# Moving GpSimd's first queue drain from ahead of the fourth slot's gathers to behind them

## The chip, the core and the metric

The kernel runs on one core of one Trainium2 chip. The metric is the device time of one launch in microseconds (us), as the median of several runs; the profile comes from one further execution. Six engines matter here: TensorE (PE, with its weight loads PEld), VectorE (DVE), ScalarE (ACT), GpSimd (POOL), SyncE (SP) for the plain DMA transfers, and the 16 DMA engines. GpSimd issues the indirect transfers (gathers and scatters) itself.

## What is computed

Attention with a sigmoid in place of the softmax, and then a mixture of eight experts that sends each token to one expert:

```python
scores = scale * q @ k.T - log(S);  attn = 1 / (1 + exp(-scores))
x = (attn @ v)                         # 8 x 448 tokens = 3584 rows of 768
e_idx = argmax(x @ w_gate)             # one expert of 8 for each token
h  = maximum(x[mask] @ w1[e], 0)       # 768 -> 1024
out[mask] = gate_w * sigmoid(x @ w_output_gate)[e] * (h @ w2[e])   # 1024 -> 768
```

All values are float32 at the interface.

## The kernel before

Attention and routing come first (about 300 us). For every token the routing writes a row of six words into a list in DRAM, sorted by expert; each expert's list is cut into tiles of 256 tokens. The second part works through these tiles, one *slot* for each: `slot(m)`, m from 0. The first `EARLY` = 3 slots take tokens whose attention ends early; the slot with m = 3, the fourth, is the last that always runs. The slots after it (same function, m > 3), the three wide slots and the two half slots of this run stand under branches.

A slot holds two layers. In layer 1 PE multiplies the 256 tokens by the expert's w1 in eight column blocks f; numbers are split into a high and a low part, so that block f takes twelve matmuls, L576 with the high and L577 with the low weights in turn, over six row pieces d = 0 to 5. In layer 2 (L601 to L603) it multiplies by w2, in four parts (t, n): two token halves t, two column halves n. From m = 3 on the last part is finished in the next slot (`finish`, at f = 6 there).

Three things are prepared while PE works, and they set the order on the other engines:

- **Tokens.** `gather` (L496 on, the DMA at L501) issues eight indirect DMAs on GpSimd, each of which fetches 128 quarter rows into `xg`, a single buffer of the pool `plain`. In slot m the gathers are for slot m + 2. `turn_x` (L558) lets DVE transpose `xg` into `xT`; it waits for all eight gathers, and the next slot's gathers wait for it. `split_x` then makes high parts on ACT and low parts on DVE (L532 and L533, from 128x512 tiles).
- **Weights.** `high_w1(k)` (ACT, L536) and `low_w1(k)` (DVE, L539), k = 0 to 2, split w1 for the next slot; piece k serves d = 2k and 2k + 1. On ACT the order at a slot's end is: high_w1(0), split_x, output (0,0), high_w1(1), output (0,1), high_w1(2), output (1,0).
- **Results.** `layer2_out` (L621) scales a part on ACT into `ys[0]` or `ys[1]` (half t), and after the second part GpSimd scatters the buffer to `out` by indirect DMA (L623). ACT's next write to the same buffer waits for that scatter to land.

Everything is in an order written by hand, engine by engine: each engine runs its own list from the top and waits only on semaphores. GpSimd's sequencer runs ahead of the GpSimd cores; a drain stops it there until the DMAs issued before have retired. `nc.gpsimd.drain()` stands in each slot after the fourth at its start (L631), in the wide slots (L685) and the half slots (L717); the first of all is in slot m = 3 (L645). Ahead of this first one GpSimd has issued 87 DMAs: two at the start, 32 that write lists, 40 gathers, seven that read lists, six scatters. In the fourth slot GpSimd also unpacks the lists of the late slots (`spread_lists`, `spread_rest`, L461 to L487), which ends just ahead of that drain.

Of the kernel before, what the change touches and what calls it, by code (L numbers as in the profile page):

```python
# [35 lines left out]
EARLY = -(-(ROWS_E - E * (TS - 1)) // TS)  # L36
# [22 lines left out]
class Kernel:  # L59
# [567 lines left out]
    def slot(self, m, side=None):  # L627
        tab, k = (self.tab_e, m + 1) if m + 1 < EARLY else (self.tab_l, m + 1 - EARLY)
        nx = self.load_slot(tab, k, self.lists(m + 1))
        if m > EARLY:  # L630
            self.nc.gpsimd.drain()  # L631
        self.split_w2(0)
        for f in range(8):
            if m > EARLY and f == 6:
                self.finish()
            self.layer1(f, m == 0 and f == 0)
            if f:
                self.high_low(f - 1)
            if f in (1, 3, 5):
                self.split_w2(f // 2 + 1)  # L640
            if side is not None and f < 7:
                next(side, None)
        self.high_low(7)
        if m == EARLY:
            self.nc.gpsimd.drain()  # L645
        self.load_w2(nx)
        self.high_w1(0)
        self.turn_x(nx)
        if m == 0:
            next(side, None)  # L650
        if m == 1:
            next(side, None)
        self.gather(self.lists(m + 2), ROWS_E if m + 2 < EARLY else NT)
        for k in range(3):
            self.split_x(nx, k)
        self.low_w1(0)
        for i, (t, n) in enumerate(((0, 0), (0, 1), (1, 0), (1, 1))):
            if i == 3 and m >= EARLY:
                self.layer2_due(self.lists(m), 1)
            else:  # L660
                ps = self.psy[(0, 1, 3)[i] if m >= EARLY else (4 * m + i) % 3]
                self.layer2(self.lists(m), t, n, self.ys[t], ps)
            if i < 2:
                self.split_w1(i + 1)
            if side is not None and i > 0:
                for _ in range(3 if m == 0 and i == 1 else 1):
                    next(side, None)
# [380 lines left out]
```

## Time and profile before

| What | us |
|---|---|
| median of three runs | 783.53 (783.46 to 785.43) |
| profiled execution | 785.01 |
| its span, first to last instruction | 783.3 |
| time around the span | 1.7 |
| PE busy | 767.6 (98%) |
| DVE / ACT / GpSimd busy | 497.8 / 488.1 / 353.9 |
| slot m = 3 (PE, layer 1 to layer 2) | about 383 to 416 |
| slot m = 4 | about 416 to 449 |

The granted clock of TensorE is 1.00 in all 20 us stretches from 300 to 740. To read the views: a timeline row has the start in us from the start of the span, the duration in us, the engine, the source line, the operation, output and input tiles, and in brackets how long the engine stood idle before and what ended it. An idle time "<-issue" is one in which the profile saw nothing to wait for. POOLq is GpSimd's sequencer, where drains are recorded.

### The profile page before, as it was taken

What the parts mean: (1) busy time and instruction counts of PE and PEld (TensorE: products, weight loads), DVE (VectorE), ACT (ScalarE), POOL (GpSimd) and SP (SyncE); (2) the same over time, 40 slices, a digit from 0 to 9 for tenths busy, and PEclk for the clock granted to TensorE, in tenths of its full rate; (3) what the DMA queues carried; (4) which work ended last, traced back from release to release, by engine and by line L of the source; (5) the groups of instructions that cost most, each with busy time, mean ns of one, the idle gap of its engine ahead of it and who ended that gap; (6) DMA issues with size and microseconds to landing.
All of it is one profiled execution on the core that took longest, in us unless ns stands there. A gap on an engine that the chain in (4) does not pass through costs nothing. (4 is left out here: it accounts for less than half of the span.)

```text
span 783.3 us, 15087 instructions
## 1 busy us (share of the span) xinstructions
PE 767.6 (98%) x5724; PEld 561.6 (72%) x5724; DVE 497.8 (64%) x800; ACT 488.1 (62%) x662; POOL 353.9 (45%) x464
## 2 busy tenths in 40 slices
PE   9999999999999999999999999999999999999896
PEld 4333433333443369899999989999899999889685
DVE  2334444443456768876786576858577685787677
ACT  5666666666668757565675565746556474675585
POOL 4003301230331676778895667255372643633522
PEclk9999999999999999999999999999999999999999
DMA  6352544445258550147666497511156655856771
GB/s 252 142 212 91 195 165 173 159 143 213 81 204 303 191 184 12 53 176 238 232 201 249 160 343 280 182 51 42 40 223 204 259 158 210 315 212 237 278 307 46
DMA packets 37616, 145.23 MB, mean 185 GB/s; under 512 B 5639, under 2 KB 7791, under 8 KB 33552
## 3 DMA queue, kind: packets, MB, share of 16 engines
q1 hardware_dynamic: 27696, 119.56, 42.6%
q0 software_dynamic: 9824, 24.46, 9.3%
q8 instruction: 51, 0.84, 0.4%
q14 instruction: 45, 0.37, 0.2%
HBM read 152.61 MB, written 23.05 MB: 224 GB/s over the span
## 5 line engine op out<-in xcount | busy, mean ns | idle before, releaser
L800 ACT ACTIVATE a<-ps,bias_s 128x896 f32<-128x896 f32 x168 | 169.1, 1008 | 96.6 <-PE ps L798 96.6
L576 PE MATMUL ps<-rounded 128*128 128x512 f32 (+1 forms) x672 | 225.9, 386 | 1.7 <-PEq L990 1.2
L501 POOL DMA_INDIRECT plain<-x_dram,lxs x122 | 181.9, 1491 | 65.2 <-issue 40.5
L577 PE MATMUL ps<-rounded 128*128 128x256 f32 (+1 forms) x672 | 184.1, 274 | 1.4 <-DVE rounded L539 1.2
L798 PE MATMUL ps<-kqv 64*64 64x448 f32 x1344 | 157.9, 541 | 0.4 <-ACT a L800 0.4
L807 PE MATMUL ps<-a,kqv 64*64 64x448 f32 x1344 | 156.8, 536 | 0.0
L601 PE MATMUL ps<-w2h,h 128*128 128x384 f32 x432 | 144.9, 335 | 0.0
L533 DVE TENSOR_TENSOR w2l<-plain,w2h 128x1536 fp32r<-128x1536 f32 x60 | 105.2, 1757 | 62.0 <-ACT w2h L532 61.4
L602 PE MATMUL ps<-w2l,h 128*128 128x384 f32 x432 | 144.4, 334 | 0.0
L603 PE MATMUL ps<-w2h,h 128*128 128x384 f32 x432 | 144.4, 334 | 0.0
L576 PEld LDWEIGHTS ps<-rounded 128*128 128x128 f32 x672 | 125.8, 187 | 25.0 <-issue 3.0
L577 PEld LDWEIGHTS ps<-rounded 128*128 128x128 f32 x672 | 127.2, 189 | 2.3 <-DVE rounded L539 2.0
L807 PEld LDWEIGHTS ps<-a,kqv 64*64 64x64 f32 x1344 | 51.6, 133 | 75.3 <-issue 74.2
L539 DVE TENSOR_TENSOR rounded<-plain,rounded 128x2048 fp32r<-128x2048 f32 x46 | 103.3, 2284 | 1.8 <-ACT rounded L536 1.8
L798 PEld LDWEIGHTS ps<-kqv 64*64 64x64 f32 x1344 | 48.7, 133 | 74.0 <-issue 60.7
L532 ACT CAST w2h<-plain 128x1536 fp32r<-128x1536 f32 x60 | 88.1, 1472 | 19.3 <-PEq L995 6.3
L584 ACT COPY gl<-ps 128x256 f32<-128x256 f32 (+1 forms) x112 | 40.3, 360 | 93.9 <-PE ps L577 87.0
L536 ACT CAST rounded<-plain 128x2048 fp32r<-128x2048 f32 x46 | 87.3, 1903 | 0.0
L601 PEld LDWEIGHTS ps<-w2h,h 128*128 128x128 f32 x432 | 81.1, 188 | 2.3 <-issue 1.8
L602 PEld LDWEIGHTS ps<-w2l,h 128*128 128x128 f32 x432 | 81.1, 188 | 0.1
L603 PEld LDWEIGHTS ps<-w2h,h 128*128 128x128 f32 x432 | 81.1, 188 | 0.0
L623 POOL DMA_INDIRECT out<-y,due x11 | 18.3, 1666 | 117.6 <-ACT gl L584 92.4
(209 smaller groups left out, 716.5 us busy)
## 6 DMA issues: line engine op xcount, KB each, us to landing
plain<-w SPq DMA_DIRECT2D x68, 768.0 KB
plain<-w SPq DMA_DIRECT2D x48, 1024.0 KB
kqv<-kqv SPq DMA_DIRECT2D x23, 1344.0 KB
x_dram<-xt SPq DMA_DIRECT2D x8, 1344.0 KB
plain<-w SPq DMA_DIRECT2D x6, 512.0 KB
plain<-x_dram,lxs POOLq DMA_INDIRECT x122, 5.0
kqv<-kqv SPq DMA_DIRECT2D x1, 896.0 KB
lst<-plain POOLq DMA_DIRECT2D x1, 726.0 KB, 7.2
```

The lines of the kernel that those rows point to most:

```text
L501: self.nc.gpsimd.indirect_dma_start(out=s["xg"][:, g], out_offset=None, in_=x4, in_offset=bass.IndirectOffsetOnAxis(ap=s["lx"][:, g:g + 1] ...
L532: self.nc.scalar.copy(hi, raw)
L533: self.nc.vector.tensor_tensor(lo, raw, r32(hi), ALU.subtract)
L539: self.nc.vector.tensor_tensor(self.w1p[1][k], self.w1r[:, 2 * k:2 * k + 2], r32(self.w1p[0][k]), ALU.subtract)
L576: nc.tensor.matmul(out, wh[d][:, c], both, start=(d == 0), stop=False)
L577: nc.tensor.matmul(ps[:, 0:n], wl[d][:, c], self.xc[:, d, 0, 0:n], start=False, stop=(d == 5))
L601: nc.tensor.matmul(ps, hh[:, f, tk], wh, start=(f == 0), stop=False)
L602: nc.tensor.matmul(ps, hh[:, f, tk], wl, start=False, stop=False)
L603: nc.tensor.matmul(ps, hl[:, f, tk], wh, start=False, stop=(f == 7))
L798: nc.tensor.matmul(ps[half[h], j, 0:S], kg[half[j], e, 0, o:o + 64], kg[half[j], e, 1], start=True, stop=True)
L800: nc.scalar.activation(at[u % 4], ps[:, :, 0:S], AF.Sigmoid, bias=self.bias_s, scale=1.0 / math.sqrt(D))
L807: nc.tensor.matmul(self.ps_o[e][h][half[j], 0:S], v[half[h], 6 if i == 3 else 3 * e + c, j], a[half[h], j], start=(i in ((0, 3 if h else 4 ...
```

## The change

Within `slot`, for m == 3 alone, the drain moves down past `load_w2`, `high_w1(0)`, `turn_x` and `gather`. Of these only `gather` issues on GpSimd, so on that engine the drain changes place with eight indirect DMAs; every other engine's list stays as it was.

```diff
         self.high_low(7)
-        if m == EARLY:
-            self.nc.gpsimd.drain()
         self.load_w2(nx)
         self.high_w1(0)
         self.turn_x(nx)
...
         self.gather(self.lists(m + 2), ROWS_E if m + 2 < EARLY else NT)
+        if m == EARLY:
+            self.nc.gpsimd.drain()
         for k in range(3):
             self.split_x(nx, k)
```

On GpSimd this is the order from the end of the list unpacking (`gl1`, `lts`) through the fourth slot's eight gathers (into `plain`, from `x_dram`) and its scatter (`out` from `y0`) to the fifth slot's first instructions. A drain is not listed, so the rows read the same in both kernels.

```order
L486 TENSOR_SCALAR gl1_105<-lts_100 32x10
L487 COPY gl1_105<-lts_100 32x10
L501 DMA plain_130<-x_dram_62,lxs_101 128x192 [waits DVE_49,Pool_49]
L501 DMA plain_130<-x_dram_62,lxs_101 128x192 x7
L623 DMA out<-y0_2465,lts_100 3584x768 [waits DMASW7_49,Activation_49]
L990 COMPARE_AND_BRANCH
L623 DMA out<-y1_2466,due_99 3584x768 [waits DMASW0_49,DMASW7_49,DVE_49,Activation_49]
```

Before, the first drain stands between L487 and the first L501; now it stands between the last L501 and the first L623. The drain of the fifth slot stands behind L990 in both.

On ACT this is the end of the fifth slot (m = 4), the same in both kernels: its high parts of w1 (L536) and x (L532 from 128x2x256), and the outputs of its layer 2 (L621).

```order
L536 CAST rounded_126<-plain_130 128x2048 [waits DMAHW2_49]
L532 CAST rounded_126<-plain_130 128x2x256 [waits DVE_49]
L532 CAST rounded_126<-plain_130 128x2x256 x2
L621 ACTIVATE y0_2465<-ps_134,lts_100 128x384 [waits DMASW7_49,PE_49]
L536 CAST rounded_126<-plain_130 128x2048 [waits DMAHW3_49]
L621 ACTIVATE y0_2465<-ps_134,lts_100 128x384 [waits PE_49]
L536 CAST rounded_126<-plain_130 128x2048 [waits DMAHW4_49]
L621 ACTIVATE y1_2466<-ps_134,lts_100 128x384 [waits DMASW0_49,PE_49]
```

Nothing moved here. DMASW7, for which the first L621 waits, is the semaphore of the fourth slot's scatter, the L623 from `y0` in the rows above.

## Rows read from the trace of the kernel before

**Rows 1.** The page's first line.
```profile
span 783.3 us, 15087 instructions
```
**Rows 2.** Timeline of PE, first block of slot m = 5.
```profile
450.18 0.39 PE L576 MATMUL ps<-rounded 128*128 128x512 f32 x1
450.72 0.39 PE L577 MATMUL ps<-rounded 128*128 128x256 f32 x1
...
451.29 0.40 PE L576 MATMUL ps<-rounded 128*128 128x512 f32 x1
452.92 0.39 PE L577 MATMUL ps<-rounded 128*128 128x256 f32 x1 [1.23 <-DVE rounded L539]
```
**Rows 3.** Timeline of DVE, ends of slots m = 3 and m = 4.
```profile
402.75 1.78 DVE L558 STREAM_TRANSPOSE plain<-plain 128x1536 f32<-128x1536 f32 x1
...
441.90 1.78 DVE L558 STREAM_TRANSPOSE plain<-plain 128x1536 f32<-128x1536 f32 x1 [7.11 <-DMA plain<-x_dram,lxs]
444.37 1.89 DVE L533 TENSOR_TENSOR rounded<-plain,rounded 128x512 fp32r<-128x512 f32 x3 [0.69 <-ACT rounded L532]
446.18 6.69 DVE L539 TENSOR_TENSOR rounded<-plain,rounded 128x2048 fp32r<-128x2048 f32 x3
```
**Rows 4.** Timeline of GpSimd, slots m = 3 and m = 4.
```profile
403.04 1.02 POOL L623 DMA_INDIRECT out<-y,lts  x1 [0.16 <-DVE h L590]
...
418.92 0.19 POOL L487 COPY gl<-lts 32x10 f32<-32x10 f32 x1
427.14 2.37 POOL L501 DMA_INDIRECT plain<-x_dram,lxs  x1 [8.03 <-issue]
...
439.10 0.94 POOL L501 DMA_INDIRECT plain<-x_dram,lxs  x1 [0.30 <-issue]
440.35 1.01 POOL L623 DMA_INDIRECT out<-y,lts  x1 [0.30 <-issue]
444.81 1.12 POOL L623 DMA_INDIRECT out<-y,due  x1 [3.46 <-ACT rounded L532]
446.24 3.08 POOL L501 DMA_INDIRECT plain<-x_dram,lxs  x1 [0.31 <-issue]
```
**Rows 5.** The drains at L645, L631 (fifth slot's), L685 (first): ns min/median/max, starts.
```profile
L645 POOLq DRAIN  x1: 8314/8314/8314, 418.0 to 418.0; - x1
...
L631 POOLq DRAIN  x1: 9682/9682/9682, 434.1 to 434.1; - x1
...
L685 POOLq DRAIN  x1: 1015/1015/1015, 661.6 to 661.6; - x1
```
**Rows 6.** Issue to landing: the fourth slot's scatter, the fifth slot's, the fourth's gathers.
```profile
DMA to landing us min/median/max: 3.1/3.1/3.1
...
DMA to landing us min/median/max: 8.0/8.0/8.0
...
DMA to landing us min/median/max: 2.6/5.3/6.3
```
**Rows 7.** Timeline of GpSimd, slot m = 1, first and last of eight gathers.
```profile
354.80 1.11 POOL L501 DMA_INDIRECT plain<-x_dram,lxs  x1
...
368.59 0.95 POOL L501 DMA_INDIRECT plain<-x_dram,lxs  x1 [0.30 <-issue]
```
**Rows 8.** Timeline of ACT, end of slot m = 4.
```profile
445.28 0.58 ACT L621 ACTIVATE y<-ps,lts 128x384 f32<-128x384 f32 x1
...
448.03 1.90 ACT L536 CAST rounded<-plain 128x2048 fp32r<-128x2048 f32 x1
```
**Rows 9.** Timeline of DVE: two low parts of w2 (L533).
```profile
422.72 1.76 DVE L533 TENSOR_TENSOR w2l<-plain,w2h 128x1536 fp32r<-128x1536 f32 x1 [0.93 <-ACT w2h L532]
...
661.93 1.76 DVE L533 TENSOR_TENSOR w2l<-plain,w2h 128x1536 fp32r<-128x1536 f32 x1 [0.89 <-ACT w2h L532]
```
**Rows 10.** Timelines of DVE and PE: slot m = 5's last low part, slot m = 6's layer 1.
```profile
479.00 2.29 DVE L539 TENSOR_TENSOR rounded<-plain,rounded 128x2048 fp32r<-128x2048 f32 x1 [0.29 <-ACT rounded L536]
...
484.70 0.39 PE L576 MATMUL ps<-rounded 128*128 128x512 f32 x1
```

## The prediction

> **What bounds the kernel now.** I began with the page: the span is 783.3 us [rows 1], and PE is busy for 98% of it, so only a place where PE stands still can be worth time. The view of waits gives PE just one wait of over 0.3 us on another engine's result from 300 us on: on DVE's low part of w1, in the first block of slot m = 5. PE's timeline shows what it costs. Undisturbed, an L577 follows its L576 after 0.23 us. Here the one at 450.72 comes 0.54 after its L576, and the next but one, at 452.92, comes 1.63 after [rows 2]: 0.31 + 1.40 = 1.7 us lost. That is the most that this stall can give back.
>
> Backwards from there. The L577 at 452.92 needs the third low_w1, the last of three L539 that run back to back from 446.18 to 452.87 [rows 3]. These stand behind split_x, and this behind turn_x, which DVE starts at 441.90 after 7.11 us of idle time, waiting for the gathers [rows 3]. The gathers are issued from 427.14 to 440.04, behind 8.03 us of idle time that the profile puts down to nothing [rows 4]. The record of GpSimd's sequencer fills that gap: the drain L645 starts at 418.0 and lasts 8.314 us, to 426.31 [rows 5]. The transpose that the gathers also wait for (turn_x of the slot before) had ended at 404.53 [rows 3]. So the drain delays the gathers, and by this chain PE loses 1.7 us.
>
> **What the drain itself costs.** GpSimd was busy until 419.11 (418.92 + 0.19) [rows 4], so the drain held it for 7.2 us, although every earlier DMA had landed: the last scatter was issued at 403.04 [rows 4]. In the first wide slot a drain, also with nothing in flight, takes 1.015 us [rows 5]; ten DMAs had been issued since the drain before it (eight gathers, two scatters). 87 DMAs and 7.2 us, ten and 1.0: both fit some 83 ns for each DMA to be retired and about 0.2 us besides. I take the drain for a walk over all DMAs since the last one. The fifth slot's drain shows that the walk need not start after the last landing: it ends at 434.1 + 9.68 = 443.78 [rows 5], 0.3 us after the scatter of 440.35 landed (+ 3.1) [rows 4, 6], although it had nine DMAs to retire.
>
> **The change part by part.** One drain changes place with eight gathers; the other lists stay.
>
> Removed: 7.85 us ahead of the gathers. They may start at some 419.3, which is 419.11 and the 0.2 us that a gather needs behind GpSimd's own copies. Issuing eight took 12.9 us here (427.14 to 440.04 [rows 4]), and 14.7 in slot m = 1 (354.80 to 369.54 [rows 7]), where each gather that met DVE's L533 took about 2.4 us. From 419 to 433 such L533 run as in that slot (the first at 422.72 [rows 9]), so I take 14.7: issued by 434.0, 6 us earlier than now. Their landing, 2.6 to 6.3 us after issue [rows 6], is then at about 436 to 439, and turn_x, split_x and the first low_w1 all run some 4 us earlier than now.
>
> Added: the same drain behind the gathers, now with 95 DMAs to retire: 7.2 x 95/87 = 7.9 us, from 434.0 to 441.9. The gathers land meanwhile, so no wait for them is left over. A gather came 0.83 us after L645's end, the fifth slot's first scatter 1.03 after L631's; with 0.8 the fourth slot's scatter L623 is issued at 442.7, where it is at 440.35 now [rows 4]. What is queued behind the drain on GpSimd is just this scatter, the fifth slot's drain, the scatter from `due` and the fifth slot's gathers; all come some 2.4 us later.
>
> Who waits for them: ACT's output (0,0) of slot m = 4 writes the buffer that this scatter reads. It runs at 445.28 now [rows 8], in its turn behind split_x, and the scatter has landed by 443.45 [rows 4, 6], so that today this wait costs nothing. With the change it lands at 442.7 + 3.1 = 445.8. ACT, ready some 4 us earlier, then stands at this output until 445.8, and high_w1(1) and high_w1(2) stand behind it. From there the chain is: 4.65 us from the output's start to the end of the second high_w1 (445.28 to 449.93 [rows 8]), 2.25 for the third low_w1 (a third of 6.69 [rows 3]), and 0.1 for two hand-overs. That is 445.85 + 7.0 = 452.85 for the L577 that runs at 452.92 now: 0.1 us gained. The end of PE's stall would be set by the scatter in place of the gathers, at nearly the same time.
>
> Behind that, the fifth slot's gathers start at 448.6 in place of 446.24 and are all issued by about 464. The last low part that depends on them ends at 481.29, and PE needs layer 1 of slot m = 6 only from 484.70 on [rows 10], so 2.4 us are covered there; without that cover they would be lost whole. From slot m = 6 on GpSimd waits for ACT, and the delay is gone. The w1 transfer that follows the first low_w1 starts earlier too, on SP's queue, and may crowd the scatter a little: I add 0.2 us for this, an estimate from landings of 3.1 and 8.0 [rows 6], at the near end, since the transfer starts about when the scatter does.
>
> Sum: -0.1 + 0.2 = +0.1 us on the profiled execution's 785.01 (783.3 of span and 1.7 around it). That execution was 1.5 us over the median of the runs, 783.53; put on the median, the forecast is 783.6 us.
>
> Bounds. Eight gathers: 12.9 to 15.7 us (446.24 on, the fifth slot's), -1.8 to +1.0. Drain: if those 7.2 us were no walk and a drain here costs 1.0, the stall ends before it begins, -1.7 in all; the other end is the second rival. Landing: 3.1 to 8.0, up to +4.9. For each I take the value nearest by place: the slot with the same DVE work, the same drain, the scatter itself.
>
> **The rivals.**
> *The drain is cheap there.* If the 7.2 us are something that stands at that point once (code that is fetched, say) and doesn't move with the drain, or if the walk gets through the old DMAs while the gathers are issued, the scatter goes out in time and the stall goes altogether: 783.53 - 1.7 = 781.8. For it: there is only one long drain to look at. Against it: the 1.0 us for ten DMAs scales to it well.
>
> *Slower: DVE shuts the drain out.* GpSimd's gathers double in time beside an L533, which reads two operands. If the walk suffers the same, it loses the 4.2 us of two-operand work that DVE has between 434 and 442 (three L533, 1.89, and one L539, 2.2 [rows 3]). The 7.2 us then hold 1.8 of such shut-out (the L533 at 422.72 [rows 9]), so the walk alone is 5.4 x 95/87 = 5.9, and with 4.2 it is 10.1: 2.2 us more than I took, 783.6 + 2.2 = 785.8. It decides if the drain takes more than about 9 us behind its last gather. Against it: the drain of 1.015 us at 661.6 [rows 5] ended at 662.6, in the middle of an L533 that began at 661.93 [rows 9]. The Trainium skill, SBUF — State Buffer, "Who interferes with whom", says that a DVE instruction with two SBUF inputs blocks a GpSimd instruction that reads SBUF, and not one that only writes. By that rule the time would be 785.8 if the walk reads SBUF, and 783.6 if it doesn't; the row at 661.6 speaks for the latter.
>
> *The scatter lands late.* With w1's transfers in the queues the next slot's scatter took 8.0 us to land [rows 6]. The same here is +4.9, 788.4. Against it: the transfer can start only after the first low_w1, at about 443, when the scatter is out.
>
> **How the numbers follow.** An exchange of one wait for another, at -1 to +1.5 us: 0.60. The stall goes (-1.7): 0.17. DVE shuts the drain out (+2.2): 0.12. The scatter lands late (up to +4.9): 0.06. Something I don't see: 0.05. 0.3%, what a measurement of this kernel can tell from no change, is 2.35 us: the band is 781.2 to 785.9. The first two cases lie inside it, so faster gets 0.04; half of the third and all of the fourth pass it, slower gets 0.13; same 0.83. The range takes in the stall's going and the shut-out drain with a little more for slow gathers: 781.8 to 786.4. The likeliest case's own range is 782.5 to 785.0.
>
> **What would show it.** Right: L645's successor, now L653, lasts about 8 us past its last gather, gathers run from 419 to 434, turn_x no longer waits 7.1 us, ACT's output (0,0) near 445 waits for DMA or for GpSimd where it now follows split_x, and PE still stands 1 to 3 us in that block. Wrong: PE without a stall there (cheap drain), a drain much over 8 us behind the last gather (shut out), or a new stall of PE in slots m = 5 or 6, which would mean that the cover there was too thin.

## The result, and the profile after

The changed kernel takes 791.9 us (median of six runs, 790.06 to 794.24) where the kernel before took 783.94 beside it: the ratio is 1.0095, with an interval of 1.0075 to 1.0115. It is slower by some 8 us, where 783.6 was forecast. The profiled execution took 794.24 us.

The page's first line of the changed kernel, the counterpart of [rows 1]:

```profile
span 792.5 us, 15087 instructions
```

**Where the time went.** I took the first L576 of each slot from PE's timeline in both traces. Up to slot m = 5 they differ by 0.4 us at most. Slot m = 5 takes 43.1 us in place of 35.2, and the slots m = 6 to 9 take 33.3 in both. So 7.9 us are lost in slot m = 5. The two spans differ by 9.2; most of the rest lies behind slot m = 9, in a part whose length varies from kernel to kernel (see a2). A slot without a stall takes 33.28 us: before, slot m = 5 lost 1.9 us, now it loses 9.8.

**GpSimd did what was forecast.** Its timeline, the counterpart of [rows 4], with the last copy, the last gather and the fourth slot's scatter, and the records of the drains L653 and L631 (ns, start), the counterpart of [rows 5]:

```profile
419.27 0.19 POOL L487 COPY gl<-lts 32x10 f32<-32x10 f32 x1
...
431.38 2.39 POOL L501 DMA_INDIRECT plain<-x_dram,lxs  x1 [0.30 <-issue]
442.67 2.81 POOL L623 DMA_INDIRECT out<-y,lts  x1 [8.90 <-issue]
```
```profile
L653 POOLq DRAIN  x1: 19635/19635/19635, 422.1 to 422.1; - x1
...
L631 POOLq DRAIN  x1: 8790/8790/8790, 442.5 to 442.5; - x1
```

The gathers end at 431.38 + 2.39 = 433.8 (forecast 434.0), the drain ends at 422.1 + 19.6 = 441.7 (441.9), the scatter is issued at 442.67 (442.7). But the issue takes 2.81 us, where it took 1.01 before [rows 4], and what follows is new: its landing, the counterpart of [rows 6], is 8.6 us in place of 3.1.

```profile
DMA to landing us min/median/max: 8.6/8.6/8.6
```

**What the scatter meets.** DVE's timeline, the counterpart of [rows 3], and that of SP, which issues the weight loads:

```profile
438.03 1.78 DVE L558 STREAM_TRANSPOSE plain<-plain 128x1536 f32<-128x1536 f32 x1 [3.04 <-DMA plain<-x_dram,lxs]
440.50 1.90 DVE L533 TENSOR_TENSOR rounded<-plain,rounded 128x512 fp32r<-128x512 f32 x3 [0.69 <-ACT rounded L532]
442.31 2.28 DVE L539 TENSOR_TENSOR rounded<-plain,rounded 128x2048 fp32r<-128x2048 f32 x1
453.71 2.29 DVE L539 TENSOR_TENSOR rounded<-plain,rounded 128x2048 fp32r<-128x2048 f32 x1 [9.12 <-ACT rounded L536]
```
```profile
444.72 0.37 SPq L522 DMA_DIRECT2D plain<-w  x1
```

The first low_w1 (L539) runs from 442.31 to 444.59, 3.9 us earlier than before [rows 3], since the gathers are earlier. It lies over the first 1.92 us of the scatter's issue, and 0.89 us are left behind it; the 35 indirect DMAs between 340 and 650 us of this trace that no L533 or L539 overlaps take 0.87 to 1.16 us to issue. The end of the low_w1 frees a piece of w1's raw buffer, and SP issues the next slot's 1 MB load into it at 444.72, 0.76 us before the scatter's issue ends at 445.48. Two answers of the DMA view, for 445.5 to 449.3 and for 449.3 to 451 (queue, packets, MB, share of 16 engines; q1 holds the plain loads, q0 GpSimd's transfers):

```profile
q1 hardware_dynamic: 243, 1.00, 94.0%
```
```profile
q0 software_dynamic: 80, 0.39, 55.6%
q1 hardware_dynamic: 29, 0.05, 8.1%
```

For 3.8 us after the end of its issue not one packet of the scatter moves; the load's 243 of 272 packets do. Then the scatter's 80 come, and it has landed at 451.3.

**Who waits for it.** ACT's timeline, the counterpart of [rows 8], and PE's first block of slot m = 5, that of [rows 2]:

```profile
439.84 1.66 ACT L532 CAST rounded<-plain 128x512 fp32r<-128x512 f32 x3 [3.51 <-DVE plain L558]
451.31 0.58 ACT L621 ACTIVATE y<-ps,lts 128x384 f32<-128x384 f32 x1 [9.81 <-DMA out<-y,lts]
451.79 1.89 ACT L536 CAST rounded<-plain 128x2048 fp32r<-128x2048 f32 x1
```
```profile
449.69 0.39 PE L576 MATMUL ps<-rounded 128*128 128x512 f32 x1
...
453.73 0.56 PE L576 MATMUL ps<-rounded 128*128 128x512 f32 x1 [3.18 <-ACT rounded L536]
456.06 0.58 PE L577 MATMUL ps<-rounded 128*128 128x256 f32 x1 [1.77 <-DVE rounded L539]
...
458.32 0.58 PE L577 MATMUL ps<-rounded 128*128 128x256 f32 x1 [0.62 <-DVE rounded L539]
```

ACT stands at output (0,0) for 9.81 us, until the landing. high_w1(1) and high_w1(2) stand behind that output on ACT, and two low_w1 behind them on DVE. The L577 of d = 4 runs at 458.32. Four pairs of 0.35 us and an offset of 0.23 after the block's start at 449.69 it would have run at 451.3: PE is 7.0 us late there. The last part of the loss is PE's own clock. The view by stretches, 449 to 466 (PE, PEld, DVE, ACT and POOL busy, granted clock, DMA share, GB/s):

```profile
449.00:454.00 5.00, 1.82 (x10) 1.38 (x9) 0.29 (x1) 2.69 (x3) 1.40 (x2) 1.00 0.33 132
454.00:456.00 2.00, 0.29 (x1) 0.00 (x0) 2.00 (x2) 1.95 (x2) 1.70 (x2) 0.51 0.59 204
456.00:464.00 8.00, 7.33 (x22) 5.95 (x23) 4.58 (x7) 2.83 (x5) 6.48 (x6) 0.50 0.84 299
464.00:466.00 2.00, 2.00 (x13) 1.68 (x11) 1.07 (x3) 1.57 (x3) 1.63 (x2) 0.94 0.97 391
```

After 3.2 us of standing still the granted clock is 0.5, the 1.2 GHz level, until about 464; before, it was 1.00 there. The slot's loss of 9.8 us is thus 7.0 of lateness and, as the remainder, 2.8 at the low clock: from 458.3 to 464, 5.7 us, PE had no further wait of over 0.25 us and ran at half its speed.

### The profile page after: what moved, and what is told of

Its sections match the earlier page's. It is cut to its first block, busy times and chain, and to the rows that moved or that the text cites. A ratio compares the mean times of both kernels' runs of the same rounds, so it can differ in the third digit from the quotient of the medians.

```text
span 792.5 us, 15087 instructions
## 1 busy us (share of the span) xinstructions
PE 772.6 (97%) x5724; PEld 565.0 (71%) x5724; DVE 498.2 (63%) x800; ACT 488.1 (62%) x662; POOL 351.8 (44%) x464
## 5 line engine op out<-in xcount | busy, mean ns | idle before, releaser
L576 PE MATMUL ps<-rounded 128*128 128x512 f32 (+1 forms) x672 | 228.8, 389 | 4.4 <-ACT rounded L536 3.2
L501 POOL DMA_INDIRECT plain<-x_dram,lxs x122 | 179.1, 1468 | 60.3 <-issue 31.9
L577 PE MATMUL ps<-rounded 128*128 128x256 f32 (+1 forms) x672 | 185.5, 276 | 2.4 <-DVE rounded L539 2.4
L576 PEld LDWEIGHTS ps<-rounded 128*128 128x128 f32 x672 | 127.4, 190 | 28.6 <-ACT rounded L536 3.5
L533 DVE TENSOR_TENSOR w2l<-plain,w2h 128x1536 fp32r<-128x1536 f32 x60 | 105.3, 1758 | 61.5 <-ACT w2h L532 60.8
L577 PEld LDWEIGHTS ps<-rounded 128*128 128x128 f32 x672 | 128.8, 192 | 3.3 <-DVE rounded L539 3.3
L539 DVE TENSOR_TENSOR rounded<-plain,rounded 128x2048 fp32r<-128x2048 f32 x46 | 103.5, 2285 | 10.9 <-ACT rounded L536 10.9
L532 ACT CAST w2h<-plain 128x1536 fp32r<-128x1536 f32 x60 | 88.2, 1473 | 18.8 <-PEq L995 6.2
L536 ACT CAST rounded<-plain 128x2048 fp32r<-128x2048 f32 x46 | 87.2, 1902 | 0.0
L623 POOL DMA_INDIRECT out<-y,due x11 | 19.1, 1736 | 123.4 <-ACT gl L584 99.9
```

What stands on the lines that cost most here:

```text
L501: self.nc.gpsimd.indirect_dma_start(out=s["xg"][:, g], out_offset=None, in_=x4, in_offset=bass.IndirectOffsetOnAxis(ap=s["lx"][:, g:g + 1] ...
L532: self.nc.scalar.copy(hi, raw)
L533: self.nc.vector.tensor_tensor(lo, raw, r32(hi), ALU.subtract)
L539: self.nc.vector.tensor_tensor(self.w1p[1][k], self.w1r[:, 2 * k:2 * k + 2], r32(self.w1p[0][k]), ALU.subtract)
L576: nc.tensor.matmul(out, wh[d][:, c], both, start=(d == 0), stop=False)
L577: nc.tensor.matmul(ps[:, 0:n], wl[d][:, c], self.xc[:, d, 0, 0:n], start=False, stop=(d == 5))
```

## The experiments

Theory 1 is the chain just read: behind the drain the scatter comes out exactly when the first low_w1 runs, which stretches its issue and lets the load go ahead of it; ACT waits for the landing, and PE for ACT. Theory 2: the lateness of everything behind the drain on GpSimd costs the time, whatever it meets. Theory 3: a long drain in that place itself hinders the transfers behind it. In all twelve kernels the slots m = 2 to 4 and 6 to 9 take 33.3 to 33.8 us (one exception, slot m = 6 of a6, is told there), so the length of slot m = 5 in the profiled execution tells the mechanism, and the ratio to the kernel before, timed on the same chip, the result:

| kernel | slot m = 5, us | ratio to before (interval) |
|---|---|---|
| before / after | 35.2 / 43.1 | 1 / 1.0095 (1.0075 to 1.0115) |
| a1, drain behind the scatter | 35.9 | 1.0013 (0.9999 to 1.0028) |
| a2, w1 loads later | 36.9 | 1.0055 (1.0036 to 1.0074) |
| a3, one more output buffer | 42.1 | 1.0098 (1.0075 to 1.0121) |
| a4, memsets for the drain | 48.3 | 1.0163 (1.0138 to 1.0187) |
| b2, after with an early drain | 33.8 | 0.9993 (0.9977 to 1.0009) |
| b1, before with an early drain | 33.28 | 0.9983 (0.9968 to 0.9997) |
| a5, three output buffers | 38.7 | 1.0044 (1.0027 to 1.0061) |
| a6, and two of `due` | 33.28 | 0.9987 (0.9964 to 1.0010) |
| d1, loads of half the size | 41.2 | 1.0098 (1.0068 to 1.0127) |
| c1, a1 and a2 together | 33.28 | 0.9976 (0.9961 to 0.9991) |

**a1: the drain behind the scatter.**

```diff
         self.gather(self.lists(m + 2), ROWS_E if m + 2 < EARLY else NT)
-        if m == EARLY:
-            self.nc.gpsimd.drain()
...
                 self.layer2(self.lists(m), t, n, self.ys[t], ps)
+                if m == EARLY and i == 1:
+                    self.nc.gpsimd.drain()
```

> The changed kernel with the drain moved once more, behind the fourth slot's scatter of its first half. Theory 1 (the scatter came out at the moment at which DVE's first low_w1 runs and frees w1's buffer for the next 1 MB load, and got behind that load): the scatter goes out at about 434, lands by 437.5, ACT's output (0,0) no longer waits, PE has no stall in the first block of slot m = 5 and its clock stays at 1.00; 782.2 us (the 783.9 of before less the 1.7 of its own stall). Theory 2 (it is the mere lateness of all that stands on GpSimd behind the long drain): the scatter from due and the fifth slot's gathers are as late as in the changed kernel, 789 to 792. Theory 3 (a long drain in that place itself hinders the transfers that follow it): the same stretch of 435 to 443 is drained, the next scatter lands late, 787 to 792.

The scatter goes out at 433.41, output (0,0) runs at 440.75 without a wait, and the first block has no stall: of the 7.9 us 7.2 are gone (43.1 to 35.9). The 1.7 us were not gained, because the next scatter meets the same fate. ACT's and DVE's timelines of a1:

```profile
453.46 0.58 ACT L621 ACTIVATE y<-ps,lts 128x384 f32<-128x384 f32 x1 [8.05 <-DMA out<-y,due]
```
```profile
453.40 0.15 DVE L611 COPY due<-lts 128x1 int32<-128x1 int32 x1 [5.06 <-DMA out<-y,due]
```

The scatter from `due`, issued at 444.52 (2.48 us, beside L539), lands only at 453.4. Output (1,0) on ACT writes its buffer, and DVE's L611 overwrites its list, so both wait for it, and PE stands for 2.1 us in the fourth block. Theories 2 and 3 had 787 to 792.

**a2: the load out of the way.** Only slot m = 5's loads go in reverse (`late` is true for that slot alone), so that the first waits for the third low_w1:

```diff
...
-        self.load_w(s, self.w1, self.w1r, range(0, 6, 2))
+        self.load_w(s, self.w1, self.w1r, range(4, -1, -2) if late else range(0, 6, 2))
...
```

> The changed kernel, but the w1 loads that SP issues in slot m = 5 go in the reverse order, so that the first of them waits for the third low_w1 instead of the first and can't start before the scatter is out. Theory 1: the scatter's issue is still stretched beside DVE (2.8 us, to 445.5), but it lands some 2 us behind that in place of 5.4; ACT's output (0,0) at about 447.5 instead of 451.3, PE's stall 3.2 us instead of 7, no fall of its clock or a short one; 785.4 us, from 784.5 to 787.5. Theories 2 and 3: the landing stays near 8.6 us and the time at 791.9, since the drain stands where it stood.

ACT's timeline and PE's waits from 440 to 480 (total, times, longest):

```profile
446.34 0.58 ACT L621 ACTIVATE y<-ps,lts 128x384 f32<-128x384 f32 x1 [6.11 <-DMA out<-y,lts]
```
```profile
PE ps L577 <- DVE rounded L539: 2.8, 2, 1.5
```

The issue is stretched as before (441.40 to 444.20), but the landing is 2.1 us behind its end in place of 5.8, and the granted clock stays at 1.00. The slot is 6.2 us shorter than in the changed kernel: that is what the load ahead of the scatter costs, the low clock included. The 1.7 us more than before are what remains of the lateness and the stretched issue. The median (787.57), just over the expected range, lies 2.2 us above what the slot explains (783.67 for the kernel before on this chip, and 1.7). From the start of slot m = 6 to PE's last matmul it takes 292.0 us in this trace and 289.4 to 292.7 in the twelve, with a granted clock of 0.74 from 740 to 750 here and 1.00 in a1. Why that part varies I did not look into.

**a3: the wait taken away, at one place.** Slot m = 4 writes its first half into `hb`:

```diff
-                self.layer2(self.lists(m), t, n, self.ys[t], ps)
+                y = self.hb[:, 0:DM] if m == EARLY + 1 and t == 0 else self.ys[t]
+                self.layer2(self.lists(m), t, n, y, ps)
```

> The changed kernel, but slot m = 4 writes its first half's outputs into a buffer of its own (hb, not in use then), so that ACT's output (0,0) doesn't wait for the late scatter. Theory 1: the scatter still lands at about 451, but output (0,0) follows split_x at 441.5, the low parts of w1 are there in time and the first block of slot m = 5 has no stall; 782.2 us, or up to 785 if ACT then stands at output (1,0) until the scatter from due has landed (about 456) and PE runs out of buffers in the fourth block. Theories 2 and 3, in which it isn't this wait: 790 to 792.

The time is what theories 2 and 3 had, and mine (up to 785) fell. But output (0,0) runs at 441.10 and the first block has no stall, as theory 1 said; the stall has moved. ACT's timeline and PE's waits:

```profile
457.37 0.58 ACT L621 ACTIVATE y<-ps,lts 128x384 f32<-128x384 f32 x1 [11.61 <-DMA out<-y,due]
```
```profile
PE ps L576 <- DVE gl L585: 5.6, 1, 5.6
```

The fifth slot's drain waits for the late scatter, so the scatter from `due` leaves at 451.86 and lands at 457.3. Output (1,0) and L611 stand there, PE runs out of buffers for 5.6 us, and its clock falls again (a mean of 0.66 from 460 to 470). I had seen this wait and priced it at 3 us.

**a4: late without a drain.** Nine memsets of `hb` stand where the drain stood:

```diff
         if m == EARLY:
-            self.nc.gpsimd.drain()
+            for _ in range(9):
+                self.nc.gpsimd.memset(self.hb, 0.0)
```

> The changed kernel without the fourth slot's drain; in its place GpSimd clears a buffer that isn't in use nine times (about 8 us of plain memsets), so that the scatter goes out as late as behind the drain, at about 442.3. The fifth slot's drain then has some 97 DMAs to retire. Theories 1 and 2: lateness is enough, the scatter gets behind the w1 load and lands some 8 us after its issue, 789 to 793 us. Theory 3 (the drain itself is what hinders): 782 to 784.

GpSimd's timeline of a4, and the landing of its fourth slot's scatter:

```profile
433.46 9.07 POOL L654 MEMSET hb<- 128x1024 f32 x9
442.69 2.25 POOL L623 DMA_INDIRECT out<-y,lts  x1 [0.16 <-issue]
455.52 2.93 POOL L623 DMA_INDIRECT out<-y,due  x1 [10.58 <-DVE rounded L539]
```
```profile
DMA to landing us min/median/max: 7.8/7.8/7.8
```

Plain memsets of the same length give the same late landing, so theory 3 falls. The time is above 793, since the fifth slot's drain now has 96 DMAs to retire and ends at 454.5, 4.0 us behind that landing (in a3, with nine, it ends at 450.9, 0.1 behind it): the scatter from `due` is late as well, as in a3.

**b2 and b1: a shorter drain in the same places.** Both add one drain at 267 us, where GpSimd is idle; b2 to the changed kernel, b1 to the one before:

```diff
             self.spread_lists(self.lr_e[1], self.lts[:, 1:EARLY], self.lxs[:, 1:EARLY])
+            self.nc.gpsimd.drain()
```

> The changed kernel with one drain more, at about 267 us, where GpSimd is idle for 5 us and 34 of the DMAs have been issued. The fourth slot's drain stands where the change put it. If a drain is a walk of some 83 ns for each DMA since the last one, it has 61 to retire in place of 95 and ends at 433.8 + 5.3 = 439.1; if its length is fixed, it ends at 441.7 as before. Theory 1: the scatter is issued at about 440, some 2.5 us earlier than in the changed kernel, and so ahead of the w1 load: it lands by 445, ACT waits for it some 3 us in place of 9.8, and the first block's stall is gone or under 1 us; what may stay is the scatter from due, which then meets the load (2.5 us of PE, as behind the drain that was moved to the end). 782.2 to 785. Theory 2, by which the loss goes with the lateness itself: about two thirds of the loss stays, 789.

> The kernel before with the same additional drain at about 267 us. If the drain is a walk, the fourth slot's drain ahead of the gathers shrinks from 8.3 us to some 5 on the sequencer, the gathers start at 424 in place of 427, everything behind them is 3 us earlier, and PE's stall of 1.7 us goes: 782.0. The scatter from due then goes out at about 441.5 and should land before the w1 load comes in (445.5); if it doesn't, ACT's output (1,0) waits and up to 2.5 us come back: 784. If the drain's length is fixed, nothing changes: 783.7.

The drains of b1 (the early one and L645), the early one retiring 34 DMAs, L645 the 53 since then; and from b2 ACT's output (0,0), the fourth slot's scatter and SP's first load:

```profile
L909 POOLq DRAIN  x1: 3837/3837/3837, 265.5 to 265.5; - x1
...
L645 POOLq DRAIN  x1: 5523/5523/5523, 420.3 to 420.3; - x1
```
```profile
446.89 0.58 ACT L621 ACTIVATE y<-ps,lts 128x384 f32<-128x384 f32 x1 [3.31 <-DMA out<-y,lts]
```
```profile
443.35 1.40 POOL L623 DMA_INDIRECT out<-y,lts  x1 [7.38 <-ACT rounded L532]
```
```profile
446.80 0.37 SPq L522 DMA_DIRECT2D plain<-w  x1
```

In b2 the drain stands where the change put it, but ends so that the scatter is issued at 443.35, relative to slot m = 5's start 1.5 us earlier than in the changed kernel (451.89 - 443.35 = 8.5, against 449.69 - 442.67 = 7.0), and in 1.40 us. It is out at 444.75, 2.05 us before SP issues the load. It lands at 446.9, the load's packets start at 447.9, and the slot takes 33.8 us. A step of about 1.5 us decides over 9 us: theory 2, by which the loss goes with the lateness, falls here. The wait of 3.3 us on ACT is harmless. b1 gains the whole stall of the kernel before (33.28), as expected of a walk.

**a5 and a6: every wait for a late scatter taken away.** a5 uses `hb` as a third buffer in turn, a6 also a second `due` (the last line), so that L611 doesn't wait either. The lines that use them are left out:

```diff
+    def ybuf(self, m):
+        a, b, c = *self.ys, self.hb[:, 0:DM]
+        return {EARLY + 1: (c, a), EARLY + 2: (b, c)}.get(m, (a, b))
...
+        due = self.due_b if m == EARLY + 1 else self.due
...
```

> The changed kernel, with three output buffers in turn in slots m = 4 and 5 (hb is the third), so that neither output (0,0) nor output (1,0) of slot m = 4 has to wait for a scatter that is queued behind the w1 load at that moment: (1,0) writes the buffer whose scatter has landed by about 451. Theory 1: the scatter still takes some 8.6 us to land, but PE's stall in slot m = 5 goes altogether and its clock stays at 1.00: 782.2. If (1,0), held until 451, still costs a little, up to 783.5. Where the wait of ACT on buffers isn't the cause: 790.

> The changed kernel with three output buffers in turn, as in the run with three, and a second buffer for what finish needs (due), so that DVE's copy L611 in slot m = 4 doesn't wait for the scatter from due either. Theory 1 (all of the loss is waits for scatters that are behind the drain and the w1 load): the scatters land as late as ever (8.6 us, and 5 for the one from due), but nobody on PE's path waits for them, PE has no stall in slot m = 5 beyond 0.5 us, the slot takes 33.3 to 33.8 us in place of 43.1 and the time is 0.997 to 1.000 of that of the kernel before. If something else also costs time there (the transfers' crowding itself, the clock), the slot stays above 35 us.

a5 missed: with no buffer in short supply, DVE's copy into `due` still waits, and L585 behind it. DVE's timeline of a5; the stretch from 450 to 460 of a6, and from its slot m = 6 DVE's transpose and the L577 of d = 4 (in a6 that line is L578, and L558 is L559):

```profile
460.89 0.15 DVE L611 COPY due<-lts 128x1 int32<-128x1 int32 x1 [8.37 <-DMA out<-y,due]
```
```profile
450.00:460.00 10.00, 10.00 (x59) 9.06 (x58) 4.67 (x8) 4.95 (x8) 4.56 (x4) 1.00 0.97 377
```
```profile
476.48 1.78 DVE L559 STREAM_TRANSPOSE plain<-plain 128x1536 f32<-128x1536 f32 x1 [5.45 <-DMA plain<-x_dram,lxs]
```
```profile
487.53 0.39 PE L578 MATMUL ps<-rounded 128*128 128x256 f32 x1 [0.42 <-DVE rounded L540]
```

In a6 the scatter still lands late (issued at 444.89, output (1,0) waits for it until 453.55), the transfers are as crowded as ever, and PE has no stall in slot m = 5 (33.28 us) and its full clock. So all of the loss in slot m = 5 is waits for these two scatters. But the lateness behind the drain is not free: the fifth slot's gathers start at 455.83, 7.0 us later against the start of slot m = 5 than before, the transpose waits for them until 476.48, and slot m = 6 takes 34.26 us, 1.0 too many.

**d1: half the load ahead.** In slot m = 5 alone, six loads of 512 KB in place of three of 1 MB:

```diff
...
+            self.load_w(s, self.w1, self.w1r, range(6), 1)
...
```

> The changed kernel with slot m = 5's three w1 loads of 1 MB cut into six of 512 KB, which wait for the same low parts. Where the scatter's packets must wait for the one load that was issued ahead of them, and the next half MB lines up behind the scatter, it lands 2 us earlier: ACT at about 449.3, slot m = 5 about 3 to 4 us shorter, 788. Where whatever SP has issued before the scatter's issue ends goes first (both halves, since SP issues them within a microsecond at 444.7 and the issue ends at 445.5), nothing changes: 791 to 793.

Neither expectation held as a whole. SP issued the halves at 447.32 and 448.01, both before the scatter's issue ended at 448.08, the second by just 0.07 us. The scatter's packets start at about 450.2, when 106 of the halves' 288 packets have moved. SP's timeline (L522 is L525 there) and the DMA view from 450.2 to 452.6:

```profile
447.32 0.35 SPq L525 DMA_DIRECT2D plain<-w  x1
448.01 0.34 SPq L525 DMA_DIRECT2D plain<-w  x1
```
```profile
q1 hardware_dynamic: 148, 0.52, 55.3%
q0 software_dynamic: 80, 0.39, 39.4%
```

The scatter then shares the engines with the rest of the load and lands 4.9 us behind its issue in place of 5.8. The slot is 1.9 us shorter (41.2), too little for the ratio to show.

**c1: the drain last and the loads later.** Both edits of a1 and a2.

> The drain behind the fourth slot's scatter, and slot m = 5's w1 loads in reverse order as well, so that the scatter from due has no load in its way either. Theory 1: that scatter is issued at about 444.5, lands by 449.5 in place of 453.4, ACT's output (1,0) waits 4 us less and the 2.5 us stall of PE in the fourth block goes: slot m = 5 takes 33.3 us, the time is 782.0, better than both kernels by what their own stalls are. If the reversed loads come too late for slot m = 6, PE stalls there and the time is 784 or more.

ACT's timeline of c1:

```profile
451.96 0.58 ACT L621 ACTIVATE y<-ps,lts 128x384 f32<-128x384 f32 x1 [3.74 <-DMA out<-y,due]
```

The scatter from `due` lands 2.1 us behind its issue in place of 6.4 in a1 (449.82 to 451.9, 447.00 to 453.4), PE has no stall, and c1 is faster than the kernel before by 0.24% (0.09 to 0.39): the 1.9 us that its slot m = 5 lost. It beats both kernels, and so, by less, does b1.

## Why the prediction was wrong

- **The bound and the gain: right.** The drain held the gathers and by them PE. b1, a6 and c1, which take the stall away, have a slot of 33.28 us, 1.9 less than before.
- **The drain as a walk: right in its length.** Behind the last work on GpSimd it takes 2.9 us for 34 DMAs (b1, 266.4 to 269.3), 4.4 for 53, 7.2 for 87, 8.0 for 95: 83 to 85 ns each. (The prediction's 83 ns and 0.2 us would give 7.4 for 87; 81 ns and 0.2 fit these rows and the 1.0 for ten.) With 61 (b2) it took 6.5 and with 96 (a1, c1) 8.7, up to 1.4 above the line. The kept traces suggest why. Drains of a1 and b2, and issue to landing of the changed kernel's last gather and of a1's scatter:

```profile
L662 POOLq DRAIN  x1: 20072/20072/20072, 423.3 to 423.3; - x1
...
L653 POOLq DRAIN  x1: 18124/18124/18124, 424.3 to 424.3; - x1
```
```profile
DMA to landing us min/median/max: 6.4/6.4/6.4
...
DMA to landing us min/median/max: 6.0/6.0/6.0
```

In the changed kernel the last gather lands at 437.8 and the drain ends 4.0 us behind that; in a1 the scatter lands at 439.4 and the drain ends at 443.4, 4.0 behind; in a4 it is 4.0 as well, in b2 about 2.5 (an estimate: the transpose that waits for the gathers starts at 440.1 and the drain ends at 442.4). That is about 42 ns for each DMA after the last landing, half of the whole price. So the drain reads as two passes, the second of which begins when the last DMA has landed: landings 4.8 and 3.9 us behind the last issue in a1 and b2, with 4.0 and 2.5 for the second pass, give 8.8 and 6.4. The fifth slot's drains, with nine DMAs, fit it less well (0 to 0.3 us behind the landing, where 0.4 would be due), and no run was made to test it. That "no wait for them is left over" was then luck: the changed kernel's last gather landed 4.0 us behind its issue, just when the first pass was through.

The rival in which DVE shuts the drain out wanted over 9 us behind the last gather; it was 8.0.

- **The ends of the gathers and of the drain, and the scatter's start: right to 0.2 us**, and so is the chain from output (0,0) to the L577, 451.31 to 458.32 = 7.0 us. The gathers' end was in part luck: they started at 419.73, 0.4 late, and took 14.0 us in place of 14.7.
- **The failed step: the scatter's landing.** I took 3.1 us, the value "nearest by place", and 0.2 for the load, "since the transfer starts about when the scatter does"; it was 8.6. The two causes stood in my rows. The prediction let gathers double beside an L533 and moved low_w1 4 us forward, but never laid that low_w1 over the scatter of the same moment: 1.01 us became 2.81. And the scatter and the load were taken to share the engines from the start, where the load, issued first, moved 243 of its 272 packets before the scatter moved one. a2 shows the load's part: with no load ahead, the scatter lands 2.1 us behind its issue in place of 5.8. What the stretch costs by itself no run separates: unstretched, the issue would have ended at 443.7, 1.0 us before the load, and the nearest run, b2, had 2.05 us between the two. The Trainium skill, SBUF — State Buffer, "Who interferes with whom", says that a DVE instruction with two SBUF inputs contends with GpSimd instructions that read SBUF. The same section infers that such an instruction leaves descriptor generation alone, since that needs the write interface. The scatter reads its offsets from SBUF (`lts`), and the measurement decides: 2.81 us, 1.92 of them beside the L539. I had weighed it for the drain and not for the scatter behind it.
- **The rival that came true was put too low and too cheap.** "The scatter lands late" got 0.06, argued away with a load "at about 443, when the scatter is out". The prediction's own rows give 444.4 for the load (446.18 and 2.23 for the first low_w1, less 4), and it came at 444.72; the scatter was out 0.76 us after that. Its price, 4.9, was the lateness alone. Measured: the L577 is 5.3 us later against its slot than before (7.0 in place of 1.7), and the low clock, which I had nowhere in the sum, adds 2.8; less the 0.2 by which the slot before lost more than its 1.7, that is 7.9.
- **The cover in slot m = 6: not tested by the changed kernel.** The fifth slot's gathers started at 453.59, 5 us later than forecast, and slot m = 6 still took 33.28 us; but PE itself came to it 8.1 us later (492.81 in place of 484.70). In a6, where PE had lost nothing in slot m = 5, gathers that were 7.0 us late cost 1.0 us there.

## What to carry to other kernels

Where a change moves a transfer that somebody waits for, lay the other engines' new times over its issue and the transfers that they set free over its landing, and take the landing from a transfer that had such a neighbour. Small shifts weigh heavily there: a microsecond and a half of the scatter's issue decided over nine here (b2 against the changed kernel). A wait that is taken away uncovers the next one on the same late transfer (output (0,0), then (1,0), then the copy into `due`), so list all its readers and overwriters before pricing it.

## What the runs showed of the hardware

- A 1 MB plain load issued 0.76 us before a scatter's issue ended kept all of the scatter's packets back for 3.8 us; shared out evenly, its 272 packets are 17 for each of 16 engines. Cut in two (288 packets, nine for each engine and half), it let the scatter in after 106 packets. The Trainium skill, DMA: Bandwidth & Descriptors, "Queues, rings and completion order", says that an engine takes turns between queues and drains a whole packet, typically some 9 to 17 descriptors, before it switches. Both runs agree with that, if a load's share of an engine is one such packet.
- PE's granted clock fell from 1.00 to 0.50, the 1.2 GHz level, where PE had stood still for 3.2 us at once (the changed kernel, low from about 454 to 464), for 5.6 (a3, 461 to 467), 2.8 and later 3.9 (a4, 453 to 463 and 470 to 473), 3.4 (a5, 464 to 468), and for 2.1 and soon after 1.8 (d1, 457 to 464). After 2.1 (a1) and after 1.5 and 1.3 (a2) it stayed at 1.00. In the changed kernel the low clock made up 2.8 of the 9.8 us.
